# Recurrent outputs of batches 2 to 4 with tokens on partitions: transposes out, row-shifting transfers in

## Chip, cores and metric

The kernel runs on one core of a Trainium2 chip. The metric is the device time of one execution in microseconds, as the median of several runs. Engine names below: TensorE (PE), VectorE (DVE), ScalarE (ACT), GpSimd (POOL), SyncE (SP, which issues the transfers here).

## The reference

Two blocks follow each other. The first is a gated linear recurrence (mLSTM) over 4 batches of 8 heads, 768 tokens, head size 40:

```python
for t in range(S):
    m_new = np.maximum(f_gate[:, :, t] + m, i_gate[:, :, t])
    f_stab = np.exp(f_gate[:, :, t] + m - m_new); i_stab = np.exp(i_gate[:, :, t] - m_new)
    C = f_stab * C + i_stab * outer(v_t, k_t)        # a 40 x 40 state for each head
    n = f_stab * n + i_stab * k_t
    y[:, :, t] = sigmoid(o_t) * (C @ q_t) / max(abs(n . q_t), 1)
```

The heads side by side give x, 768 tokens x 320. The second block is u = x + Re(FFT over tokens and features of x), a layer norm, an MLP of width 1280 with ReLU, and out = u + MLP. All in 32-bit floats.

## The kernel before

**Chunks.** Tokens go in 6 chunks of 128 for each batch. Batch 1 (b = 0 in the code) works on whole chunks. Batches 2 to 4 (`plan_halves`) split each chunk in two halves of 64 tokens, so that all products of 64x64 or less run on four tiles of TensorE side by side. For each such chunk: scores of keys against queries (`halves_scores`), products of keys and weighted values which update the state (`halves_to_state`, `halves_add`), weights times scores (`halves_weigh`, VectorE), then the outputs: products from the state (`halves_from_state`) and from the chunk itself (`halves_from_chunk`, two turns with a small ScalarE copy, `halves_between`, in between).

**Outputs before.** A product has its stationary operand loaded into the array and its moving operand streamed. Before the change the stationary operand of an output is a 64-column slice of the state or a 41-column slice of the values (40 values and the column for n), and the moving one the 64 queries or weights. So the outputs lie in PSUM with head features on partitions and tokens along the row. `halves_gather` (ScalarE, `mlstm_heads`) copies them to SBUF, `halves_turn` turns them with four 128x128 transposes on TensorE (L681), and `mlstm_finish` (L684, VectorE) divides by the denominator, applies the output gate (tanh of half, `mlstm_tanh`) and writes x.

**Order of tokens.** The transform over tokens first folds token t with its mirror S - t: chunk pairs (0,5), (1,4), (2,3) (`mix_fold`). One chunk of each pair must lie backwards and shifted by one row. Before, these are chunks 2, 4 and 5 (`BACKWARDS`); the copy in `mlstm_heads` does the reversal and the shift, for free, as tokens lie along the row there. Rows whose token belongs to another chunk are copied one at a time (`h_first`).

**What sets the order.** The order is written by hand: `at(slot, phase, fn)` puts each step in a slot and a phase (EVAC 0, FILL 1, MAIN 2, FILL_PE 3), and the program is emitted in that order, so every engine works off its own instructions in it. For chunk c of a batch that starts at slot s0, s = s0 + 3c; scores stand at s, outputs at s + 3, the turn at s0 + (7, 10, 13, 16, 19, 19)[c], the finish one slot later. The MLP of batch 1 fills slots 31 to 62 (its products L1022, L1013, L1147), that of the next ones 32 slots each (`mlp_block` L1084, L1089; `mlp_out_pair` L1203). While a batch is in its MLP, the next one is in its recurrence. Second-layer weights arrive as 64-bit floats and are turned to 32 bits in five pieces (`Piece`: take and join on VectorE, convert on ScalarE) during batch 1's MLP.

**Queues and places.** All transfers are issued by SP in program order. Score tiles W have 3 buffers, gate inputs `so` 4. PSUM: scores and state products share one pair of banks, outputs and turned outputs another (`side(0)`, `side(1)`).

Of the kernel before, what the change touches and what calls it, by code (L numbers as in the profile page):

```python
# [10 lines left out]
FP = mybir.dt.float32  # L11
# [4 lines left out]
OP = mybir.AluOpType  # L16
# [24 lines left out]
BACKWARDS = (2, 4, 5)  # L41
PAIRS = ((0, 5), (1, 4), (2, 3))
ORDER = (0, 5, 1, 4, 2, 3)
M_INIT = -1.0e30
# [8 lines left out]
def kernel(  # L53
# [87 lines left out]
    def gates(gp):  # L141
# [44 lines left out]
        for t in hT_bufs + Cd_bufs:  # L186
            nc.gpsimd.memset(t, 0.0)
# [115 lines left out]

        def maxima_out():
            nc.sync.dma_start(out=M_d.rearrange("c i p t -> p c i t"), in_=M[0:BH].rearrange("p c (i t) -> p c i t", i=2))

        def halves_of_chunks(step):
# [8 lines left out]
            elif step == 1:  # L316
# [3 lines left out]
                nc.sync.dma_start(out=G_d[:, H:].rearrange("c p t -> p c t"), in_=g[H:BH])  # L320
# [12 lines left out]
            else:  # L333
                pt, pd = late["p2"]
                nc.vector.tensor_copy(out=colT[:, :, 1, H:], in_=pt[:, :, H:])  # L335
                nc.vector.tensor_copy(out=decB[:, NP:], in_=pd[:, NP:])

        at(12, FILL + 0.7, maxima_out)
        at(1, FILL + 0.2, parts, last)
# [9 lines left out]
        for n, (s, phase) in enumerate(((16, FILL + 0.2), (18, FILL + 0.3), (19, FILL + 0.4), (21, FILL_PE + 0.5),  # L349
                                        (26, FILL + 0.8))):  # L350
            at(s, phase, halves_of_chunks, n)
# [90 lines left out]
    def mlstm_queries(b, c):  # L442
        return slice(LH if b > 0 and c == 0 else 0, L)
# [40 lines left out]
    def mlstm_mask(b, c):  # L484
        for i in range(2):
            W = chunks[b, c].W[i * LH:(i + 1) * LH]
            nc.gpsimd.affine_select(out=W, in_=W, compare_op=OP.is_ge, fill=0.0, base=0, pattern=[[0, H], [1, LH]],  # L487
# [71 lines left out]
    def mlstm_heads(b, c, ph, parts=False):  # L559
# [3 lines left out]
        if b > 0:  # L563
            hT, before = (t.rearrange("p (hip m) t -> p hip m t", hip=2) for t in (hT, before))
        every, first, later = (tuple([slice(None)] * (len(ph.shape) - 1) + [t]) for t in
                               (slice(0, L), slice(0, 1), slice(1, L)))
        if c in BACKWARDS:
            nc.scalar.copy(out=hT[later], in_=backwards(ph, L - 1, L - 1))
            if c > TG:
                nc.scalar.copy(out=hT[first], in_=ph[first])  # L570
            else:
                nc.gpsimd.tensor_copy(out=k.hT[:, :, 0:1], in_=h_first)
        else:
            for r in (slice(hip * 64, hip * 64 + D1) for hip in range(2)) if parts else (slice(0, L),):
                nc.scalar.copy(out=hT[r], in_=ph[r])
            if c == 0:
# [869 lines left out]
```

## Time and profile before

| | us |
|---|---|
| median of 13 runs | 408.28 (403.96 to 411.09) |
| the profiled execution | 406.44 |
| its span in the profile | 404.7 |
| PE busy in 0 to 62.4 us: batch 1's recurrence and mix | 57.35 |
| PE busy in 62.4 to 117.7: batch 1 MLP, first layer; batch 2 recurrence | 51.70 of 55.30 |
| 117.7 to 171.7: second layer; batch 2 mix; batch 3 recurrence begins | 54.00 of 54.00 |
| 171.7 to 211.2: batch 2 MLP, first layer; batch 3 recurrence ends | 37.88 of 39.50 |
| 211.2 to 261.1: second layer; batch 3 mix; batch 4 recurrence begins | 48.84 of 49.90 |
| 261.1 to 300.4: batch 3 MLP, first layer; batch 4 recurrence ends | 37.80 of 39.30 |
| 300.4 to 341.0: second layer; batch 4 mix | 40.23 of 40.60 |
| 341.0 to 404.7: batch 4 MLP | 60.36 of 63.70 |

The profile is of one execution; its times are from the span's start. Busy times of TensorE are modelled from pipelined records, so the distance from one start to the next tells more than a record's duration. A wait is put down to the semaphore that came last.

### The profile page before, as it was taken

How to read it: one execution, taken by the hardware profiler on the slowest of the kernel's cores; microseconds unless marked ns; L12 is line 12 of the kernel's file. 1: busy time of each engine (PE TensorE's matmuls, PEld its weight loads, DVE VectorE, ACT ScalarE, POOL GpSimd, SP SyncE). 2: the span in 40 equal slices, each digit the busy share in tenths (PEclk: the TensorE clock that was granted, in tenths of full speed). 3: DMA queues.
4: the chain of work that ended last, by engine and by line, in shares of the span. 5: the costliest groups of instructions: out<-in, count | busy, mean ns of one | idle time of the engine just before them, and what ended most of it. 6: DMA issues, size and time to landing. Idle time of an engine off the chain costs nothing.

```text
span 404.7 us, 10669 instructions
## 1 busy us (share of the span) xinstructions
PE 388.2 (96%) x4246; PEld 283.8 (70%) x4246; DVE 280.2 (69%) x669; ACT 181.6 (45%) x510; POOL 131.6 (33%) x228
## 2 busy tenths in 40 slices
PE   8999999999899999998999999989999999999996
PEld 6877555556567677765559998856469997556996
DVE  8789976799748448576965579966764785436652
ACT  6987258587551242553472334644440023455000
POOL 5656314398952441240162424430220000020000
PEclk9999999999999999999999999999999999999999
DMA  7889599489555244365010644300000000000000
GB/s 211 283 233 324 118 237 266 128 250 246 152 150 144 64 138 124 92 188 153 0 43 3 168 112 144 101 3 2 0 2 16 18 35 32 0 2 0 32 34 32
DMA packets 23836, 43.29 MB, mean 107 GB/s; under 512 B 5076, under 2 KB 12972, under 8 KB 23660
## 3 DMA queue, kind: packets, MB, share of 16 engines
q1 hardware_dynamic: 23788, 42.63, 37.0%
q8 instruction: 33, 0.54, 0.6%
q14 instruction: 15, 0.12, 0.1%
HBM read 38.49 MB, written 4.12 MB: 105 GB/s over the span
## 4 chain that ended last, share of the span: by engine, by line
PE 80%; DVE 10%; issue 3%; ACT 3%; DMA 2%; POOL 1%; SPq 0%; POOLq 0%; DVEq 0%; ACTq 0%
PE po L1203 17%; PE pm L1084 17%; PE po L1147 8%; PE pm L1089 5%; PE pm L1022 5%; PE ph L491 4%; PE ps L491 3%; PE pu L901 3%; PE pz L870 2%; PE ph L681 2%; DMA qk<-in_qkT 2%; PE pm L1013 1%; PE put L944 1%; PE pz L858 1%; PE ph L532 1%
## 5 line engine op out<-in xcount | busy, mean ns | idle before, releaser
L1153 DVE SCALAR_TENSOR_TENSOR x<-po,rstd,x 128x160 f32<-128x160 f32 (+1 forms) x69 | 27.0, 395 | 38.0 <-PE po L1203 35.3
L1093 DVE TENSOR_TENSOR h<-h,pm 128x384 f32<-128x384 f32 x60 | 30.7, 550 | 31.1 <-PE pm L1084 17.1
L1084 PE MATMUL pm<-uT,w_sb 128*128 128x384 f32 x90 | 37.3, 501 | 0.2 <-DVE uT L1072 0.2
L464 ACT ACTIVATE W<-W,colT 128x64 f32<-128x64 f32 x144 | 37.4, 341 | 0.0
L1147 PE MATMUL po<-w_sb,h 128*128 128x320 f32 x120 | 34.4, 435 | 0.0
L629 POOL TENSOR_TENSOR C<-C,decB 128x164 f32<-128x164 f32 x30 | 17.1, 571 | 51.9 <-DVE C L638 47.7
L487 POOL TENSOR_SCALAR_AFFINE_SELECT W<-W 64x512 f32<-64x512 f32 x36 | 29.0, 806 | 15.2 <-ACT W L464 8.5
L1022 PE MATMUL pm<-uT,w_sb 128*128 128x384 f32 x80 | 29.9, 500 | 0.4 <-issue 0.2
L474 POOL TENSOR_TENSOR qg<-qk,Gb 128x512 f32<-128x512 f32 (+1 forms) x21 | 28.4, 1351 | 1.4 <-DMA Gb<-G_d 1.3
L1147 PEld LDWEIGHTS po<-w_sb,h 128*128 128x128 f32 x120 | 22.2, 190 | 9.4 <-issue 0.6
L1203 PE MATMUL po<-T,S 128*128 128x160 f32 x180 | 28.0, 302 | 0.3 <-DVE x L1153 0.3
L1203 PEld LDWEIGHTS po<-T,S 128*128 128x128 f32 x180 | 25.5, 190 | 1.8 <-DVE x L1153 0.5
L1203 PE MATMUL po<-w_sb,h 128*128 128x160 f32 x180 | 26.4, 301 | 0.0
L1203 PEld LDWEIGHTS po<-w_sb,h 128*128 128x128 f32 x180 | 25.1, 190 | 1.2 <-DVE x L1153 0.3
L1089 PE MATMUL pm<-uT,w1t_sb 64*128 64x384 f32 x120 | 25.4, 510 | 0.0
L968 POOL TENSOR_TENSOR t<-rstd 128x6 f32<-128x6 f32 x12 | 3.1, 256 | 65.3 <-DVE v L962 64.8
L1084 PEld LDWEIGHTS pm<-uT,w_sb 128*128 128x128 f32 x90 | 15.5, 189 | 12.5 <-DVE h L1093 3.6
L1140 ACT ACTIVATE h<-h 128x384 f32<-128x384 f32 x45 | 23.1, 520 | 2.0 <-DVE h L1093 2.0
L670 ACT COPY warm<-ph 1x1 f32<-1x1 f32 x18 | 2.6, 147 | 46.3 <-PE ph L491 42.8
L480 POOL TENSOR_TENSOR vw<-kvt,colT 128x328 f32<-128x328 f32 x23 | 18.6, 809 | 13.6 <-DVE colT L335 10.8
L949 ACT COPY uT<-put 128x384 f32<-128x384 f32 x24 | 11.1, 475 | 26.1 <-PE put L944 26.1
L937 ACT ACTIVATE uc<-x 128x384 f32<-128x384 f32 x24 | 14.6, 617 | 14.8 <-DVE x L929 14.8
(233 smaller groups left out, 878.8 us busy)
## 6 DMA issues: line engine op xcount, KB each, us to landing
kvt<-in_kv SPq DMA_DIRECT2D x24, 336.0 KB
qk<-in_qkT SPq DMA_DIRECT2D x48, 160.0 KB
raw<-in_w SPq DMA_DIRECT2D x10, 640.0 KB
Gb<-G_d SPq DMA_DIRECT2D x36, 128.0 KB
W<-M_d SPq DMA_DIRECT2D x36, 128.0 KB
so<-in_o SPq DMA_DIRECT2D x24, 160.0 KB
out<-x SPq DMA_DIRECT2D x24, 160.0 KB
ds_sb<-in_dft_s SPq DMA_DIRECT2D x1, 1155.0 KB
```

Of the source, the lines that this page charges most:

```text
L464: nc.scalar.activation(out=k.W[:, h, :], in_=M, func=AF.Exp, scale=-1.0, bias=colT[:, c, 0, b * H + h:b * H + h + 1])
L474: nc.gpsimd.tensor_tensor(out=k.qg[:, :, t], in0=k.qk[:, 0, :, t], in1=k.Gb[:, :, t], op=OP.mult)
L487: nc.gpsimd.affine_select(out=W, in_=W, compare_op=OP.is_ge, fill=0.0, base=0, pattern=[[0, H], [1, LH]], channel_multiplier=-1)
L491: nc.tensor.matmul(out, w, x, start=start, stop=True, skip_group_check=True)
L1022: nc.tensor.matmul(k.pm[i], w1_sb[:, ch, f0:f0 + L], u[2 * ch], start=(ch == 0 and not ahead), stop=(ch == 1 and ahead), skip_group_check= ...
L1084: nc.tensor.matmul(bank, w, u, start=start, stop=True, skip_group_check=True)
L1089: nc.tensor.matmul(bank, block(w1t_sb, i)[rows], mlp_u(gr, 1)[rows], start=False, stop=True, skip_group_check=True)
L1093: nc.vector.tensor_tensor(out=h, in0=h, in1=bank, op=OP.add)
L1140: nc.scalar.activation(out=h, in_=h, func=AF.Relu, scale=-1.0)
L1147: nc.tensor.matmul(k.po, hidden(gr, f)[:, i * L:(i + 1) * L], w2_sb[:, f, :], start=(f == 0), stop=(f == NFF - 1))
L1153: nc.vector.scalar_tensor_tensor(out=u, in0=po, scalar=k.rstd[:, c:c + 1], in1=u, op0=OP.mult, op1=OP.add)
L1203: nc.tensor.matmul(po, a[:, f], w[:, f], start=start and f == 0, stop=f == half - 1, skip_group_check=True)
```

## The change

For batches 2 to 4 the operands of the output products are exchanged: queries or weights are stationary (64 columns), the state or the values move (41 columns). The outputs then lie with tokens on partitions, and `mlstm_finish` reads them directly: the ScalarE copy, the four transposes and the second place in PSUM are gone. The finish stands at s + 4 (chunk 2 of batch 3: s + 5).

The reversal along tokens can no longer be done by a copy. The queries of backward chunks are loaded reversed (the host's layout), with maxima, decays and output gates reversed to match; the maxima and decays by copies on GpSimd and transfers to memory in four parts each. The backward chunks are now 0, 1 and 3, for batch 1 too. The shift by one row is made by transfers from SBUF to SBUF, 112 rows and 15 rows, in the new `halves_rows`, with single rows beside them. For odd head pairs the two halves of keys and values change places, so the state's sum reads its two banks crosswise.

Also: batches 3 and 4 start their recurrence at slots 53 and 83 (50 and 82), the output gates load a slot earlier, weights times scores stand earlier in batch 2, one piece of second-layer weights is converted a chunk earlier, two additions of the mix move.

```diff
-BACKWARDS = (2, 4, 5)
+BACKWARDS = (0, 1, 3)
...
 def halves_from_state(b, c):
-    k.ph = side(0)
...
-    product(k.ph[e * 64:(e + 1) * 64, hip, m, t], k.C[i][r, p * D1:p * D1 + LH], k.qg[r, p, t],
-            m == 0 and i == (c == 0))
+    k.ph = banks["heads"][:, :, 0:NP * D1].rearrange("p hip (m d) -> p hip m d", d=D1)
...
+    product(k.ph[t, hip, p, :], k.qg[r, p, t], k.C[i][r, p * D1:(p + 1) * D1], p == 0)
 def halves_from_chunk(b, c, turn):
...
-    product(k.ph[e * 64:e * 64 + n, hip, m, r], k.v[r, h * D1:h * D1 + n], k.W[r, h, :], False)
+    product(k.ph[queries(c, i), hip, p, :], k.W[rows(j), h, :], k.v[rows(j), h * D1:(h + 1) * D1],
+            2 * c + i == 0 and m == turn == 0)
-def halves_gather(b, c):
...
-def halves_turn(b, c):
-    k = chunks[b, c]
-    px = side(0 if c == NT - 1 else 1)
-    for p in range(NP):
-        nc.tensor.transpose(px[:, p // 2, p % 2], k.hT[:, p, :], ident)
-    k.px = px
 def mlstm_finish(b, c):
...
+    k.x = k.so if b > 0 and c in BACKWARDS else xs[b][:, c, 0:DM]
+def halves_rows(b, c):
+    x, y = xs[b][:, :, 0:DM], chunks[b, c].x
+    def move(out, in_):
+        nc.sync.dma_start(out=out, in_=in_)
+    if c == 2:
+        nc.gpsimd.tensor_copy(out=x[0:1, 1], in_=x[0:1, 2])
+        nc.gpsimd.tensor_copy(out=x[0:1, 2], in_=x[0:1, 0])
+        move(x[0:1, 0], chunks[b, 1].x[L - 1:L])
+    elif c in BACKWARDS:
+        n = L - L // 8
+        move(x[1:n + 1, c], y[0:n])
+        move(x[n + 1:L, c], y[n:L - 1])
+        if c != 1:
+            move(x[0:1, c], y[L - 1:L])
 def plan_halves(b, s0, stride=3):
...
-    at(s, FILL, mlstm_load_o, b, c)
+    at(s - 1, FILL, mlstm_load_o, b, c)
-    at(s + 1, MAIN + 0.7, halves_weigh, b, c)
+    at(s + 1, FILL + 0.55 if b == 1 and c > 0 else MAIN + 0.7, halves_weigh, b, c)
...
-    at(s + 4, FILL - 0.6, halves_gather, b, c)
-    at(s + 4, FILL + 0.35, mlstm_tanh, b, c)
-    t = s0 + (7, 10, 13, 16, 19, 19)[c]
-    at(t, FILL_PE + 0.5, halves_turn, b, c)
-    at(t + 1, MAIN + 0.55, mlstm_finish, b, c)
+    at(s + 3, FILL_PE + 0.6, mlstm_tanh, b, c)
+    at(s + (5 if (b, c) == (2, 2) else 4), FILL + 0.3 if b == 1 else MAIN + 0.55, mlstm_finish, b, c)
+    at(s + 6, FILL - 0.6, halves_rows, b, c)
...
-plan_batch(2, 50, 83, s_mlp + 2 * MLP_SLOTS)
-plan_batch(3, 82, 115, s_mlp + 3 * MLP_SLOTS)
+plan_batch(2, 53, 83, s_mlp + 2 * MLP_SLOTS)
+plan_batch(3, 83, 115, s_mlp + 3 * MLP_SLOTS)
...
-when += [((33, 0.7), (35, 0.7), (36, 0.6))] + [((s, 0.7), (s + 1, 0.7), (s + 2, 0.6)) for s in (36, 39, 42, 45)]
+when += [((33, 0.7), (34, 0.3), (34, 0.6)), ((34, 0.7), (35, 2.7), (36, 0.6))]
+when += [((s, 0.7), (s + 1, 0.7), (s + 2, 0.6)) for s in (36, 39, 42)]
```

## The prediction

> **What bounds the kernel now.** I read the page's busy shares first, then the busy time by stage, then who TensorE waited for, then TensorE's instructions in order of time around a few recurrence chunks, and last VectorE's in the stage in which it is fullest.
>
> ```profile
> PE 388.2 (96%) x4246; PEld 283.8 (70%) x4246; DVE 280.2 (69%) x669; ACT 181.6 (45%) x510; POOL 131.6 (33%) x228
> PE 80%; DVE 10%; issue 3%; ACT 3%; DMA 2%; POOL 1%; SPq 0%; POOLq 0%; DVEq 0%; ACTq 0%
> ```
> ```profile
> 62.40:117.70 55.30, 51.70 (x945) 31.19 (x943) 43.33 (x85) 37.21 (x112) 38.55 (x53) 1.00 0.74 204
> 117.70:171.70 54.00, 54.00 (x702) 39.40 (x700) 34.17 (x94) 18.74 (x61) 19.48 (x27) 1.00 0.39 110
> 171.70:211.20 39.50, 37.88 (x314) 21.53 (x306) 30.29 (x75) 21.34 (x59) 12.90 (x29) 1.00 0.34 94
> 211.20:261.10 49.90, 48.84 (x847) 45.80 (x846) 36.09 (x97) 19.27 (x62) 18.74 (x28) 1.00 0.39 110
> 261.10:300.40 39.30, 37.80 (x311) 21.51 (x304) 27.77 (x72) 19.38 (x50) 10.56 (x26) 1.00 0.02 5
> ```
> The columns after the stretch are its length, then busy PE, PEld, DVE, ACT, POOL, the granted clock and DMA. These five stages hold all the work that the change touches in batches 2 to 4: call them B, C, D, E, F. TensorE has no idle time in C and 1.1 to 3.6 us in the others, so a microsecond of TensorE work taken away is nearly a microsecond off the span, unless another engine was about as late. Its waits:
> ```profile
> PE ph L491 <- DVE x L703: 3.9, 5, 1.3
> PE ps L491 <- issue: 1.0, 1, 1.0
> PE pm L1013 <- issue: 0.8, 1, 0.8
> PE ph L491 <- ACT warm L670: 0.7, 1, 0.7
> PE ph L491 <- DVE W L643: 0.5, 1, 0.5
> ```
> The first line is D, E and F; the other four are B. In B, VectorE's order of time shows no idle time at all from 76.2 to 108.1 us: there it is as late as TensorE.
>
> **What a chunk costs on TensorE.** One chunk in order of time (start, duration, instruction; a 32-bit product leaves two records, a transpose one), then the same kinds in other shapes:
> ```profile
> 169.87 0.69 PE L491 MATMUL ph<-qg,C 40*64 40x64 f32 x32
> 170.38 0.41 PE L491 MATMUL ph<-W,kvt 64*41 64x64 f32 x16
> 170.61 0.65 PE L491 MATMUL ps<-qk 40*64 40x64 f32 x32
> 171.07 0.49 PE L491 MATMUL ps<-vw,kvt 64*40 64x41 f32 x32
> 171.38 0.41 PE L491 MATMUL ph<-W,kvt 64*41 64x64 f32 x16
> 171.72 1.56 PE L1084 MATMUL pm<-uT,w_sb 128*128 128x384 f32 x4
> 173.12 0.60 PE L681 MATMUL ph<-ident,h 128*128 128x128 f32 x4
> 173.55 0.49 PE L1084 MATMUL pm<-uT,w_sb 128*128 128x384 f32 x1
> ```
> ```profile
> 211.69 0.63 PE L491 MATMUL ps<-vw,kvt 64*64 64x41 f32 x32
> 212.25 0.54 PE L1203 MATMUL po<-w_sb,h 128*128 128x160 f32 x2
> ```
> The step from start to start is the price, since a record's own duration overlaps the next. Read: 16 products from the state 0.51 us, 8 from the chunk 0.23 us (0.34 us where full-array work follows, so that switch costs 0.11), and four transposes 0.43 us.
>
> **Removed: the turns.** 18 chunks x 4 transposes at 0.43 to 0.44 us a chunk: **7.9 us**, all between full-array products, so all on the path. With them go ScalarE's copies of the heads, 18 at 0.585 us and 12 small ones at 0.18, 12.7 us of an engine that is 45% busy: nothing by themselves, only less in front of its other copies.
>
> **Exchanged: stationary and moving operand.** 264 products from the state and 288 from the chunk now stream 41 columns and not 64. The favourable end: time goes with the moving columns. Scores against state products of this trace are 0.46 us at 64 columns and 0.31 at 41, 9.6 ns a product; 552 x 9.6 ns = 5.3 us saved. [...] The nearest row decides: the first chunk's state update already has the new shape, 64 stationary and 41 moving columns. It takes 212.25 - 211.69 = 0.56 us, less the switch 0.11: 0.45 us for 16. So narrow streaming buys little where 64 columns are loaded. From the state 0.51 -> 0.45 for 16, 16.5 times: 1.0 us; from the chunk 0.23 -> 0.225 for 8, 36 times: 0.2. I take **1.2 us** saved (ends -2.7 and +5.3).
>
> **Moved: the finish.** Before, products from the state of chunk c wait for the finish of chunk c-2, planned one slot ahead (for the last chunk less: slot s0+17 against the start of s0+18), and that finish waits for the turn. Now the finish of c-1 stands at s0+3c+1 and the products at s0+3c+3: two slots (2.0 us each in D and F, 2.8 in B, 4 and more in C and E) for five VectorE instructions, 0.16+0.17+0.20+0.64+0.49 = 1.7 us. The five waits, 3.9 us, should go. What is late next there is VectorE itself: in D from 171.8 to 179.5 us it has one gap of 0.24. I count two thirds, **2.6 us** (ends 0 and 3.9).
>
> **Weight conversion a chunk earlier.** In B, VectorE works off one conversion of 5 us per chunk without a gap. The new plan starts one of them in VectorE's idle stretches between 68 and 74 us (4.7 us in two waits), so VectorE is about 5 us less late, more than the about 2 us that TensorE loses there in work. Of B's 3.6 us of idle TensorE I count **0.7** (ends -1 and 3). Its load isn't later than now: the buffer is freed a chunk earlier as well. Weights a chunk earlier on VectorE (the product with the scores) are part of the same cover.
>
> **Added, at no cost, and what covers it.** Per batch nine row transfers: 112 and 15 rows for three chunks, single rows beside. None is on TensorE's path unless the fold waits for it. Tightest is chunk 3: issued at slot s0+15, folded at s0+18, so three slots, 5.9 us in D and F, 8.3 in B. From issue to landing, the trace has a gate transfer of 128 KB 1.8 us after its issue, and at the other end a 640 KB weight piece 6.3 us (59.92 to 66.20). 143 KB is nearest the first. Cost 0; at the far end under 1 us in D and in F. [...] On SP's queue that is 27 issues more, and six for the turned maxima and decays, at about 0.4 us: 1.2 us a chunk beside 4.4 us of issues in a period of 7.4. They wait for a finish planned two slots earlier; behind them stand the loads of a chunk four ahead, which already wait for buffers (W for TensorE, 35 us in all), and output stores. GpSimd: six one-row copies of 320 (a row of 161 takes 0.31, so 0.6 us each), less 6 small copies; four copies of the maxima in batch 1, about 1.5 us, ahead of a gate product which is done at 31.6 and used at 36.7 us; half-row swaps 0.7 us inside a wait of 2.4; two decay copies ahead of loads that have over 10 us. VectorE: two more small copies in its gap near 52 us. If these covers were gone, 1 to 2 us. Batches 3 and 4 start their recurrence three and one slots later; the last fold step then stands two and four slots ahead of the transforms, so this moves work and adds none.
>
> **Sum.** 7.9 + 1.2 + 2.6 + 0.7 = 12.4 us of the profiled 404.7 us span: 392.3. The profiled execution took 406.44, 1.74 over its span: 394.0. It was a run 0.45% under the median of 13 (408.28), so on the median's scale 394.0 x 408.28/406.44 = **395.8 us**.
>
> **Rivals.**
> 1. Streaming is what counts, and every wait goes: 7.9 + 5.3 + 3.9 + 2 = 19.1, span 385.6, time 389.1. Against it stands the 0.45 us row. Chance 0.14.
> 2. VectorE and GpSimd set the pace in B and D. For it: VectorE has no gap over 31 us in B, GpSimd none from 84 to 93; in D it takes over chunk 3's work, and 30.3 + 2.9 us in a stage of some 36 is 92%. Then the eight chunks or so of B and D return nothing, and the waits in D come back under other names: 7.9 x 10/18 + 0.6 + 1 = 6 us, span 398.7, time 402.2. Against it: the conversion brought forward. Chance 0.16.
> 3. Slower: the head outputs now have one place, which only VectorE's finish frees, for every one of 18 chunks; before, ScalarE's copy freed it, and the place read by VectorE was another. If VectorE is late each time as in its worst case now (1.27 us), TensorE idles 18 x 1.27 = 22.9 us. Span 404.7 - 9.1 - 3.9 + 22.9 = 414.6, time 418.2. It decides from (9.1 + 3.9)/18 = 0.72 us a chunk beyond the two slots. For it: rival 2's fullness. Against: in C and E two slots are 8 us. Chance 0.08.
>
> My forecast has 0.62, its own range 392 to 400. The range of 389 to 403.5 takes in most of rivals 1 and 2 and leaves out about 0.2. A measurement of this kernel can tell about 0.5% from no change: faster by more 0.87, within it 0.05 (rival 2 with costs of rival 3), slower 0.08.
>
> **What would show it.** Right: no transposes from the heads and about 8 us less of TensorE work between 62 and 300 us; no wait of head products for the finish above 1 us in all; products from the state still near 0.45 us for 16; stages C and E each about 2 us shorter, D and F about 3; nothing changed after the last batch's MLP starts. Wrong: state products at 0.33 us (rival 1); VectorE without gaps in B and D with TensorE waiting for its sums or weights (2); a wait for the finish at most chunks (3); VectorE or GpSimd waiting for row transfers ahead of the folds.

## The result

The kernel after takes **403.3 us** (median of 11 runs, 401.87 to 404.04) against 406.83 for the kernel before on the same chip; the ratio is 0.9908, interval 0.988 to 0.9936. So it is faster, by 3.5 us and not by the 12.4 forecast. (Each run below has its ratio to the kernel before on its own chip, so runs are compared by their ratios.) The profiled execution has a span of 400.5 us, 4.2 less than before.

Names in the profile's lines: `ps` and `ph` are the places in PSUM of scores and of head outputs, `pm` and `po` those of the MLP's two layers, `C` the state, `W` the weights, `uc` the normalised copy of a row of the mix, `x` a residual. First the page of the kernel after, engine totals and the chain's shares:

```profile
PE 382.5 (96%) x4174; PEld 278.4 (70%) x4174; DVE 278.9 (70%) x671; ACT 171.7 (43%) x481; POOL 131.9 (33%) x237
...
PEclk9999999979999999999999999999999999999999
...
PE 71%; DVE 17%; issue 4%; DMA 4%; ACT 2%; POOL 1%; SPq 0%; DVEq 0%; POOLq 0%; ACTq 0%
```

TensorE is busy 5.7 us less and ScalarE 9.9 us less: the turns and the copies are gone. (In work it is about 8.3 us less on TensorE: a stretch at half clock, shown below, made its products 2.6 us longer.) But TensorE's share of the chain of work fell from 80% to 71% and VectorE's rose from 10% to 17%: more of the time now passes through VectorE. And the row of the granted clock has a 7 in its ninth slice (80 to 90 us) where before there were only nines. By stage, the columns as before:

```profile
62.71:117.30 54.59, 50.95 (x865) 30.50 (x863) 44.51 (x89) 32.36 (x96) 33.51 (x50) 0.94 0.69 189
117.30:169.07 51.77, 51.77 (x629) 37.41 (x621) 31.24 (x86) 16.19 (x54) 16.73 (x23) 1.00 0.46 126
169.07:207.47 38.40, 36.72 (x418) 20.82 (x413) 28.66 (x76) 20.16 (x57) 15.49 (x33) 1.00 0.55 136
207.47:256.65 49.18, 47.64 (x714) 43.92 (x713) 35.28 (x100) 18.10 (x58) 16.63 (x25) 1.00 0.38 105
256.65:294.54 37.89, 36.40 (x415) 20.59 (x413) 28.40 (x72) 18.74 (x51) 15.11 (x32) 1.00 0.10 26
```

The borders are the same events as before (start of the first scores of batch 2, of the MLP's second layer of batch 1, of the first layer of batch 2, and so on), where before they lay at 62.44, 117.70, 171.72, 210.33, 261.14 and 299.55. B, of 55.26 us, became 54.59, and that although the first scores of batch 3 and the state products behind them (1.07 us) left it for C. Its clock is 0.94. The idle time of TensorE, length less busy time, is 3.60 us in B before and 3.64 after; over B to F together it is 7.8 before and 8.4 after. None of it went. TensorE's longest waits of the kernel after:

```profile
PE po L1237 <- DVE x L1187: 2.5, 3, 1.1
PE ps L519 <- DVE C L667: 1.9, 1, 1.9
PE ph L519 <- ACT warm L699: 1.6, 2, 1.3
PE pm L1118 <- DVE h L1127: 1.3, 2, 1.0
...
PE ph L519 <- DVE x L720: 1.0, 1, 1.0
```

The last line is the wait for the finish: 3.9 us before, 1.0 now. The four lines above it weren't there before, or were under 0.8 us. Lines two and three are stage B, and the place where they lie shows more than the sum. TensorE there, in order of time (start, duration, instruction, idle time before it and who ended it):

```profile
81.00 0.42 PE L519 MATMUL ph<-kvt,W 64*64 64x41 f32 x16
83.29 0.69 PE L519 MATMUL ps<-qk 40*64 40x64 f32 x32 [1.86 <-DVE C L667]
83.80 0.49 PE L519 MATMUL ps<-vw,kvt 64*40 64x41 f32 x32
85.64 0.67 PE L519 MATMUL ph<-kvt,W 64*64 64x41 f32 x16 [1.35 <-ACT warm L699]
...
86.93 4.82 PE L1056 MATMUL pm<-uT,w_sb 128*128 128x384 f32 x8
```

The scores of chunk 3 (c = 2) wait 1.86 us for VectorE's state add (L667), the second turn of chunk 2's outputs (L519, eight products of two records) waits 1.35 us for ScalarE's one-element read of the heads (`warm`, L699). Behind them eight products of 384 columns take 4.82 us; in run 11 below the same eight take 2.75, and the whole stretch from 85.64 to 91.69, 6.05 us here, takes 3.43 there. The clock in steps of 2 us tells why:

```profile
82.00:84.00 2.00, 0.71 (x53) 0.71 (x57) 1.71 (x5) 1.37 (x3) 0.69 (x2) 1.00 0.87 194
84.00:86.00 2.00, 0.65 (x46) 0.54 (x35) 2.00 (x2) 1.96 (x8) 2.00 (x2) 0.57 0.82 298
86.00:88.00 2.00, 2.00 (x17) 1.53 (x14) 1.90 (x5) 0.82 (x3) 1.91 (x2) 0.50 0.88 233
88.00:90.00 2.00, 2.00 (x4) 1.01 (x3) 1.50 (x3) 1.37 (x6) 1.16 (x2) 0.50 0.91 215
90.00:92.00 2.00, 2.00 (x6) 0.97 (x6) 1.74 (x6) 0.88 (x2) 0.20 (x1) 0.72 0.98 369
92.00:94.00 2.00, 2.00 (x9) 0.94 (x6) 2.00 (x2) 1.94 (x6) 2.00 (x2) 1.00 1.05 241
```

The column of the clock (after POOL) reads 1.00, 0.57, 0.50, 0.50, 0.72, 1.00. At the same place the kernel before has two shorter waits, and its clock stays 1.00:

```profile
81.03 0.44 PE L491 MATMUL ph<-W,kvt 64*41 64x64 f32 x16 [0.54 <-DVE W L643]
83.02 0.43 PE L491 MATMUL ph<-W,kvt 64*41 64x64 f32 x16 [0.75 <-ACT warm L670]
```

And what the two engines were waited for were doing, VectorE and then ScalarE:

```profile
79.06 0.68 DVE L672 TENSOR_TENSOR W<-ps,W 128x512 f32<-128x512 f32 x1
79.66 0.81 DVE L420 SCALAR_TENSOR_TENSOR e<-raw,e 128x640 uint32<-128x640 uint32 x1
80.39 0.82 DVE L422 SCALAR_TENSOR_TENSOR m<-raw,m 128x640 f32<-128x640 uint32 x1
81.25 0.82 DVE L426 TENSOR_TENSOR w_sb<-m,e 128x640 f32<-128x640 f32 x1
82.10 0.49 DVE L406 TENSOR_SCALAR e<-raw 128x640 uint32<-128x640 uint32 x1
82.51 0.49 DVE L408 TENSOR_SCALAR m<-raw 128x640 uint32<-128x640 uint32 x1
82.92 0.32 DVE L667 TENSOR_TENSOR C<-C,ps 128x164 f32<-128x164 f32 x1
```

```profile
82.63 0.83 ACT L413 ACTIVATE e<-e,ebias 128x640 uint32<-128x640 uint32 x1 [3.31 <-DVE e L406]
...
84.95 0.60 ACT L971 ACTIVATE uc<-x 128x384 f32<-128x384 f32 x1
85.45 0.13 ACT L699 COPY warm<-ph 1x1 f32<-1x1 f32 x1
```

VectorE has done the finish of chunk 1 and the weighing (L672), then joins one weight piece (L420, L422, L426) and takes the next (L406, L408) before it adds the state at 82.92. ScalarE stood 3.31 us ahead of its conversion (L413) for that take, and the one-element read is queued behind it in the same engine. One late engine holds up TensorE twice, by two ways. What has changed in VectorE's order is the place of the finish. The last instruction of the finish of chunk 1, before and after:

```profile
88.39 0.49 DVE L703 TENSOR_TENSOR x<-ph,so 128x320 f32<-128x320 f32 x1
78.65 0.49 DVE L720 TENSOR_TENSOR so<-ph,so 128x320 f32<-128x320 f32 x1
```

It is done nearly 10 us earlier, and the weighing behind it stands ahead of the weight piece, where before it stood behind (80.29 us).

### The profile page after: what moved, and what is told of

Same layout as the page of the kernel before. It is cut to its first block, busy times and chain, and to the rows that moved or that the text cites. A ratio compares the mean times of both kernels' runs of the same rounds, so it can differ in the third digit from the quotient of the medians.

```text
span 400.5 us, 10588 instructions
## 1 busy us (share of the span) xinstructions
PE 382.5 (96%) x4174; PEld 278.4 (70%) x4174; DVE 278.9 (70%) x671; ACT 171.7 (43%) x481; POOL 131.9 (33%) x237
## 4 chain that ended last, share of the span: by engine, by line
PE 71%; DVE 17%; issue 4%; DMA 4%; ACT 2%; POOL 1%; SPq 0%; DVEq 0%; POOLq 0%; ACTq 0%
PE po L1237 18%; PE pm L1118 15%; PE po L1181 8%; PE pm L1056 5%; PE pm L1123 4%; PE ph L519 4%; PE pu L935 3%; PE ps L519 2%; DMA Gb<-G_d 2%; PE pz L904 1%; DMA W<-M_d 1%; PE pz L892 1%; DVE h L1127 1%; PE put L978 1%; DVE so L716 1%
## 5 line engine op out<-in xcount | busy, mean ns | idle before, releaser
L652 POOL TENSOR_TENSOR C<-C,decB 128x164 f32<-128x164 f32 x30 | 15.7, 524 | 75.4 <-DVE C L667 64.2
L1118 PE MATMUL pm<-uT,w_sb 128*128 128x384 f32 x90 | 37.7, 506 | 2.1 <-DVE h L1127 1.3
L1056 PE MATMUL pm<-uT,w_sb 128*128 128x384 f32 x80 | 31.4, 530 | 0.1
L515 POOL TENSOR_SCALAR_AFFINE_SELECT W<-W 64x512 f32<-64x512 f32 x36 | 27.0, 749 | 13.4 <-ACT W L491 11.7
L1118 PEld LDWEIGHTS pm<-uT,w_sb 128*128 128x128 f32 x90 | 15.5, 189 | 16.4 <-DVE h L1127 7.5
L1123 PE MATMUL pm<-uT,w1t_sb 64*128 64x384 f32 x120 | 23.4, 508 | 0.0
L983 ACT COPY uT<-put 128x384 f32<-128x384 f32 x24 | 11.1, 476 | 27.7 <-PE put L978 27.7
L1056 PEld LDWEIGHTS pm<-uT,w_sb 128*128 128x128 f32 x80 | 15.2, 204 | 10.7 <-issue 3.2
```

The costliest lines, as they stand in the source:

```text
L1056: nc.tensor.matmul(k.pm[i], w1_sb[:, ch, f0:f0 + L], u[2 * ch], start=(ch == 0 and not ahead), stop=(ch == 1 and ahead), skip_group_check= ...
L1118: nc.tensor.matmul(bank, w, u, start=start, stop=True, skip_group_check=True)
L1123: nc.tensor.matmul(bank, block(w1t_sb, i)[rows], mlp_u(gr, 1)[rows], start=False, stop=True, skip_group_check=True)
```

## The experiments

Theory 1: TensorE's work was freed as forecast, and much of what is missing was lost in stage B, where the finish now stands earlier on VectorE, ahead of weight conversions and state adds; the other part went to waits for VectorE in stages E to G (G is what lies behind F). Rivals: the turns had been worth less than 7.9 us; the row transfers cost; the lower clock is the loss; the new places of the conversions are.

**1. The conversion schedule of before.** Of the change, only the weight pieces' slots are put back.

```diff
-    when += [((33, 0.7), (34, 0.3), (34, 0.6)), ((34, 0.7), (35, 2.7), (36, 0.6))]
-    when += [((s, 0.7), (s + 1, 0.7), (s + 2, 0.6)) for s in (36, 39, 42)]
+    when += [((33, 0.7), (35, 0.7), (36, 0.6))] + [((s, 0.7), (s + 1, 0.7), (s + 2, 0.6)) for s in (36, 39, 42, 45)]
```

> The changed kernel with the weight conversions at their old slots. Theory 1: conversion and finish both moved forward fill VectorE between 69 and 88 us; the scores of chunk 3 wait 1.9 us for its state sum, the second turn 1.4 for ScalarE behind a conversion, and TensorE then runs some 7 us at half clock. Then the waits shrink below 1.5 us together, no dip of the clock, and the time falls 3 to 5 us below the changed kernel's. Theory 2: the earlier finish alone fills VectorE, or the lateness comes later in the stage: within 1 us of the changed kernel, and the dip stays or moves.

Measured: 403.02 us, ratio 0.9925 (0.9893 to 0.9957), no difference from the kernel after. The waits are there under the same names (2.9 us in three for `warm`, 1.4 for the state add), and the clock is 0.50 to 0.54 from 84 to 90 us. The change had moved the last four pieces, not one, to earlier slots (34, 36, 39, 42 for 36, 39, 42, 45); that was neither the loss nor the gain of 0.7 us that the forecast had for it.

**2. The mix additions of before** (slots 4, 4, 5, 6, 8, 9 in batches 3 and 4).

```diff
-            add = [s_mix + c for c in ((4, 4, 5, 6, 7, 7) if b == 1 else (4, 5, 5, 6, 8, 9))]
+            add = [s_mix + c for c in ((4, 4, 5, 6, 7, 7) if b == 1 else (4, 4, 5, 6, 8, 9))]
```

> The changed kernel with the second addition of the mix back at its old slot (batches 3 and 4). Theory 1: that move puts two additions of 2.6 us each between finish, weights and residuals, and makes TensorE wait 1.5 us in the second layer of batch 2 and 1.0 in that of batch 3: 2 to 2.5 us less than the changed kernel. Theory 2: the waits are VectorE's total work there and come back at the next residual: within 0.7 us.

Measured: 403.97 us, ratio 0.9949 (0.993 to 0.9968): not better. The two waits for a residual in stage E and G (1.09, 1.01) give way to one of 2.72 us in E and one of 0.25 in G, as before the change: so the wait in G came from the moved addition, while in E it only took another shape.

**3. The kernel before without its turns.** This prices the removed work alone; the finish reads whatever lies there, and the place is set to zero once at the start.

```diff
-            nc.tensor.transpose(px[:, p // 2, p % 2], k.hT[:, p, :], ident)
+            pass
```

> The kernel before, leaving out the four transposes of each chunk of batches 2 to 4; the finish reads what lies in PSUM. Theory 1 (TensorE bounds, transposes are worth their 7.9 us): 7 to 11 us below the kernel before, as the finish no longer waits for a turn either. Theory 2 (VectorE and GpSimd are about as late): less than 4 us, with TensorE's idle time up by the rest.

Measured: 399.96 us, ratio 0.985 (0.9805 to 0.9894), 6.4 us less than the 406.38 of before on the same chip; span 397.3. The turns were worth four fifths of their TensorE time in the old schedule. By stage, B got 1.3 us shorter, C and D 3.2, E and F 2.1; of the 72 transposes of the kernel before 16 lie in B, 32 in C and D and 24 in E and F, which at 0.43 us for four is 1.7, 3.4 and 2.6. So the term of 7.9 us isn't what failed.

**4. The turns put back as useless work into the kernel after** (four transposes a chunk into unused columns of the heads' place, in the old slots).

```diff
+            at(s0 + (7, 10, 13, 16, 19, 19)[c], FILL_PE + 0.5, more_turns, b, c)
```

> The changed kernel with four transposes of an idle tile added for each chunk, at the slots of the old turns, into PSUM that nobody reads. Theory 1: the 14 chunks outside the stage of the conversions cost 0.44 us each: 6 to 8 us above the changed kernel. Theory 2: TensorE has room, under 4 us above it.

Measured: 433.94 us, ratio 1.0682 (1.0639 to 1.0725), far outside both. The waits say that the edit did something else as well:

```profile
PE ph L703 <- DVE x L724: 10.6, 6, 2.5
PE ph L703 <- DVE so L724: 8.4, 5, 3.1
```

L703 is the added transpose. It writes the place that the finish reads, and waits for it 11 times, 19.0 us. As a price of the turns it is inconclusive. It does show that a second writer of the heads' one place is dear; 12 of the 31 us that the run lost are not explained.

**5. The state add first.** In batch 2 the second state add of a chunk stands directly behind the weighing, ahead of the weight piece.

```diff
-                at(s + 1 + i, FILL - 0.2, halves_add, b, c, i)
+                at(s + 1, FILL + 0.56, halves_add, b, c, 1) if b == 1 and c > 0 and i else at(s + 1 + i, FILL - 0.2, halves_add, b, c, i)
```

> The kernel after, with one order changed: in batch 2 the second state add of chunks 2 to 6 stands on VectorE ahead of a weight piece's last three operations and of the next piece's first two, directly behind the chunk's weighing. Theory 1 (what cost the gain is a queue on VectorE: the scores of chunk 3 of batch 2 waited 1.86 us, at 83.29, for the state add, which stood behind those five operations): this wait goes. But the next wait in line, TensorE's second turn behind ScalarE's one-element read of the heads (1.35 us), stands behind the same piece's conversion on ScalarE, so part of it comes back there: I expect the two waits together to fall from 3.2 us to 1 to 3 us, and the time by 0 to 3 us against the kernel after (403.3). If the two together stay over 2 us the half clock behind them stays too. Rival (the waits are only slack that TensorE's clock limit would take anyway): the wait goes, and the time stays within 0.5 us.

Measured: 404.15 us, ratio 0.9947 (0.9918 to 0.9975). That is the order of the kernel before (80.29 and 80.89 us there). The wait for the state add is gone, and all of it and more came back in the other: TensorE stood 4.86 us for `warm` at 88.15 (I had expected 1 to 3 for both), with the clock at 0.5 until 92. (The 2 us in the expectation, over which the half clock was to stay, are an estimate of mine between the 1.29 us of waits before, at a clock of 1.00, and the 3.2 us of the kernel after, at 0.50.) With one of the two queues mended, the other takes it all.

**6. Both, and three weight pieces a slot later,** their conversion behind `warm`.

```diff
-    when += [((s, 0.7), (s + 1, 0.7), (s + 2, 0.6)) for s in (36, 39, 42)]
+    when += [((s, 0.7), (s + 1, 2.7), (s + 2, 0.6)) for s in (37, 40, 43)]
```

> The kernel after with the same state adds ahead, and the last three weight pieces one slot later, their conversion on ScalarE behind the one-element read of the heads and their last three operations on VectorE behind the chunk's finish, weighing and state add. Theory 1 (the queues on VectorE and ScalarE made the two waits of 1.86 and 1.35 us, and TensorE's idle time then brought the half clock that cost another 2.1 to 2.5 us): both waits fall under 0.5 us, the granted clock in 84 to 92 us is 1.00, and the time falls by 4 to 6 us against the kernel after, to 397.5 to 399.5. Theory 2 (VectorE is simply full from 69 to 88 us, and work put later comes due elsewhere): the waits appear at another place of the same stage, the gain is under 2 us.

Measured: 401.82 us, ratio 0.99 (0.9875 to 0.9925), no clear gain on the kernel after (0.988 to 0.9936): closer to theory 2. Both waits are gone, but the piece ahead of them was late as well, and with it a row of the mix that stands behind it, so TensorE waited 2.02 us for ScalarE's normalised copy (`put` <- `uc`) at 78.66, with the clock at 0.5 from 80 us. The piece had to move too (run 9).

**7. Useless products in the waits**, so that TensorE doesn't stand still.

```diff
+            if (b, c) == (1, 1):
+                at(s + 3, FILL_PE + 0.7, fill, 5)
+                at(s + 3, FILL_PE + 2.9, fill, 4)
```

> The kernel after, with nine products of 160 columns without use (about 0.30 us each, into unused columns of the heads' bank) in the queue of TensorE: five between the first turn of chunk 2 of batch 2 and the scores that wait 1.86 us, four ahead of the second turn that waits 1.35 us. The waits stay, but TensorE works through them. Theory 1 (idle TensorE makes the clock drop to half): the granted clock from 84 to 92 us is 1.00 and not 0.5, the eight products there take 2.75 us and not 4.8, and the time falls by 1.5 to 2.5 us against the kernel after, although nine products were added. Theory 2 (the half clock comes from something else, as a power limit): the clock drops as before, and the time stays or rises by up to 0.5 us.

Measured: 406.74 us, ratio 1.0013 (0.9992 to 1.0034). The products stood behind `warm`, which reads the same place, and waited 4.2 us for it: the place again, as in run 4. It says nothing of the clock; run 11 does it again in another place.

**8. No row transfers.**

```diff
-        k.x = k.so if b > 0 and c in BACKWARDS else xs[b][:, c, 0:DM]
+        k.x = xs[b][:, c, 0:DM]
...
-            at(s + 6, FILL - 0.6, halves_rows, b, c)
```

> The kernel after without the row-shifting transfers and row copies of batches 2 to 4 (12 transfers for each batch but the last rows, and the two copies of one row); the finish writes the backward chunks straight into the residual, so their tokens lie one row off, and the output isn't the reference's. Theory 1 (the row transfers are hidden, and what was lost was lost on VectorE): within 0.7 us of the kernel after. Theory 2 (the transfers delay what follows: the residual's additions, or they hold up SP's queue and slow VectorE's operations): faster by 1.5 us or more.

Measured: 406.41 us, ratio 1.0006 (0.9969 to 1.0043). It wasn't within 0.7 us, it was 1% slower than the kernel after. TensorE's waits in B are the same to the hundredth (1.86 and 1.35 us). The span is 3.7 us longer: 0.9 ahead of B, which the edit doesn't touch, a wait of 0.75 for a finish in D, and what is new in E:

```profile
247.30 0.49 DVE L720 TENSOR_TENSOR x<-ph,so 128x320 f32<-128x320 f32 x1 [1.96 <-DMA out<-x]
```

The finish now writes a backward chunk straight into the residual's tile, whose earlier contents are still on the way out; it waited 1.96 us for that store, and TensorE 2.37 us for the residual behind it (0.45 in the kernel after). So the run doesn't price the transfers alone. But in the kernel after no engine is put down as waiting for one of them, so they cost nothing that shows, and in E the detour through another tile, which they need, spares a wait.

**9. Four weight pieces later.** Run 6 with its earlier state adds (the edit of run 5), and the piece that stood ahead of the late mix row moved as well.

```diff
-    when += [((33, 0.7), (34, 0.3), (34, 0.6)), ((34, 0.7), (35, 2.7), (36, 0.6))]
-    when += [((s, 0.7), (s + 1, 0.7), (s + 2, 0.6)) for s in (36, 39, 42)]
+    when += [((33, 0.7), (34, 0.3), (34, 0.6))]
+    when += [((s, 0.7), (s + 1, 2.7), (s + 2, 0.6)) for s in (37, 40, 43, 46)]
```

> The kernel after with the second state add of chunks 2 to 6 of batch 2 directly behind the weighing, and the last four weight pieces (one more than in the run with three moved) three slots later, from the slot behind the chunk's finish on, their conversion on ScalarE behind the one-element read. No weight operation is then left on VectorE between 75 us and the second state add, and the residual that was late when three were moved (the wait of 2.02 us on ScalarE's normalised copy) has no piece ahead of it. Theory 1 (where the weight pieces stand on VectorE and ScalarE decides the waits of this stage, and with them the clock): the waits on the state add, on the one-element read and on the normalised copy fall under 1 us in sum, the granted clock is 1.00 between 80 and 96 us, and the time falls by 3.5 to 6 us against the kernel after, to 397.5 to 400. Theory 2 (VectorE is full in this stage wherever they stand): the waits come again at another place of the stage, 402 to 404 us.

Measured: 398.57 us, ratio 0.9775 (0.9717 to 0.9833), inside theory 1's window and clear of the kernel after (0.988 to 0.9936). The state adds alone had gained nothing (run 5); the pieces alone were not tried. Stage B ends at 114.9 us and not at 117.3. The same windows as above, in steps of 4 us:

```profile
80.00:84.00 4.00, 4.00 (x139) 2.89 (x138) 2.10 (x8) 3.31 (x10) 3.53 (x5) 1.00 0.85 185
...
88.00:92.00 4.00, 4.00 (x136) 2.63 (x136) 3.90 (x7) 2.76 (x9) 3.10 (x4) 1.00 0.94 268
108.00:112.00 4.00, 2.37 (x53) 1.45 (x52) 3.06 (x9) 1.36 (x5) 3.69 (x6) 1.00 0.93 219
112.00:116.00 4.00, 4.00 (x25) 1.88 (x24) 3.72 (x11) 1.99 (x7) 2.16 (x6) 0.57 0.96 246
```

TensorE has no idle time from 80 to 92 us and the clock is 1.00 there. The last of the moved pieces makes a smaller stall at 108 (TensorE busy 2.37 of 4 us), and the clock falls behind it.

**10. The finish behind the residual**, on top of run 9, for batches 3 and 4.

```diff
-            at(s + (5 if (b, c) == (2, 2) else 4), FILL + 0.3 if b == 1 else MAIN + 0.55, mlstm_finish, b, c)
+            at(s + (4 if b == 1 else 5), FILL + (0.3 if b == 1 else -0.5), mlstm_finish, b, c)
```

> As the run before it, and in batches 3 and 4 each finish stands on VectorE behind the residual of the next slot and not ahead of it. In the kernel after TensorE waited 1.09 us at 234.35, 0.45 at 246.75 and 1.01 at 321.03 for a residual that stood behind a mix add, a finish (1.7 us) and a weighing. Theory 1 (the finish in that place makes these waits): they go, and the time is 1.5 to 2.5 us under that of the run before it. Rival (the first product of the next chunk then waits for the later finish, since the heads have one place): a wait of the first state product on the finish of 0.5 to 1 us a chunk takes their place, and the time stays or rises by up to 4 us.

Measured: 403.63 us, ratio 0.9905 (0.9869 to 0.9941), 1.3% above run 9: the rival's side. The finish is later, but the residual stands in the middle of the slot (phase MAIN) and so still behind it: the waits for it stayed (3.1 us in three), and those for the finish grew from 2.0 to 3.0. Run 13 moves it really behind.

**11. Useless products in the waits, placed so that they wait for nothing.**

```diff
+                at(s + 3, FILL_PE + 0.3, fill, "heads", 256, 160, 6)
+                at(s + 3, FILL_PE + 2.9, fill, "scores", 420, 92, 6)
```

> The kernel after with products without use in TensorE's queue, this time ahead of the one-element read so that none waits for it: six of 160 columns (0.30 us each) into unused columns of the heads' bank ahead of the scores that wait 1.86 us at 83.29, and six of 92 columns (about 0.17 us each) into unused columns of the scores' bank ahead of the second turn that waits 1.35 us. Theory 1 (idle TensorE brings the half clock of 86 to 91 us, which made the eight products there take 4.8 us and not 2.75): the clock stays 1.00 through 80 to 92 us, those products take 2.8 us, and the time falls by 1.5 to 2.5 us against the kernel after although twelve products were added. Theory 2 (it has another cause): the clock falls to 0.5 as before, and the time is within 0.5 us or up to 1 us longer.

TensorE in order of time, L700 being the added products and L1064 the eight that took 4.82 us:

```profile
82.65 1.90 PE L700 MATMUL ph<-rest 128*128 128x160 f32 x12
84.59 0.69 PE L519 MATMUL ps<-qk 40*64 40x64 f32 x32
...
85.53 1.57 PE L700 MATMUL ps<-rest 128*128 128x92 f32 x12
87.04 0.44 PE L519 MATMUL ph<-kvt,W 64*64 64x41 f32 x16
...
87.79 2.75 PE L1064 MATMUL pm<-uT,w_sb 128*128 128x384 f32 x8
...
104.68 0.32 PE L519 MATMUL ph<-kvt,W 64*64 64x41 f32 x5 [1.54 <-issue]
```

Measured: 403.34 us, ratio 0.9892 (0.984 to 0.9944). The granted clock of the profiled execution is 1.000 (0.50 from 84.4 to 91.0 us in the kernel after), and the eight products take 2.75 us and not 4.82. So idle time did bring the half clock here, as theory 1 has it. But the time isn't shorter, where I had expected 1.5 to 2.5 us: stage B ends at 118.7 us. TensorE was 1.2 us ahead of the kernel after behind these products (91.31 us against 92.53). Then it stood 0.51 us for `warm` at 95.7, and 1.54 us at 104.7 in the middle of a group of eight products, a pause for which the profile names no engine ("issue"). So filling the waits gained nothing here, but how much the half clock costs by itself stays open: the added products took longer than the waits (1.94 and 1.51 us from start to start, against 1.86 and 1.35), and the last pause may have nothing to do with VectorE.

**12. The last four weight pieces not converted.**

```diff
-        for (s, phase), fn in zip(w, (p.take, p.convert, p.join)):
+        for (s, phase), fn in zip(w, (p.take, p.convert, p.join) if n < 6 else ()):
```

> The kernel after with the last four pieces of the second layer's weights not converted at all: their places hold zeros, so the output isn't the reference's; their loads stay. About 14 us of VectorE and 6 us of ScalarE work are gone from the stage between 73 and 100 us, and nothing else moves. Theory 1 (with this work there, the earlier finish made VectorE late, and that cost what the turns had freed): the stage ends 5 to 6.5 us earlier, the clock stays 1.00, and the time is 397 to 398.5 us, near that of the kernel before without its turns (399.96, a gain of 6.4 us). Theory 2 (the waits come from the order of the chunks, not from the weight work): under 2 us.

```profile
62.70:111.50 48.80, 48.37 (x868) 28.79 (x864) 27.65 (x70) 27.66 (x89) 31.43 (x52) 1.00 0.84 225
111.50:163.20 51.70, 51.70 (x624) 37.40 (x620) 31.25 (x86) 16.12 (x54) 16.48 (x22) 1.00 0.43 121
```

Measured: **396.13 us**, ratio 0.972 (0.9672 to 0.9768). Stage B lasts 48.8 us in place of 54.6 and TensorE idles 0.43 us in it; stage C is as long as in the kernel after (51.7). The two waits (3.2 us) and the time lost to the half clock (2.6) make up these 5.8 us. It is an upper bound on what the order can give, since 17 us of VectorE work left B here (44.5 to 27.7), and that could have helped the kernel before too.

**13. The finish really behind the residual** for three chunks of batch 4, on top of run 9.

```diff
+            f = (s + 5 if (b, c) == (2, 2) else s + 4, FILL + 0.3 if b == 1 else MAIN + 0.55)
+            at(*((s + 5, MAIN + 0.2) if b == 3 and c < 3 else f), mlstm_finish, b, c)
```

> The kernel with the state add first and four weight pieces later (398.57 us), and the finishes of chunks 1 to 3 of batch 4 now really behind the residual of the slot that follows (in the run that meant to do it they moved one slot, but still stood ahead of the residual, whose place is in the middle of the slot). Theory 1 (finish ahead of residual makes the waits in stage E): the waits of 1.09 us and 0.45 us for a residual in this stage go, the time falls by 1 to 1.5 us. Rival (VectorE is full there, or the first state product of the next chunk waits for the later finish): waits of the same size under another name, within 0.5 us, or up to 2 us longer.

Measured: 401.51 us, ratio 0.9845 (0.9808 to 0.9883), not better than run 9. The waits of 1.09 and 0.45 us in E go, and there come 0.84 and 0.58 for residuals, 0.60 for a mix addition and, at the border to F, 0.92 for the finish. The rival holds: VectorE is busy 15.2 of the 16 us between 232 and 248, and what is put last there is late.

**14. As 13, and the last weight piece behind the finish of its slot.**

```diff
-    when += [((s, 0.7), (s + 1, 2.7), (s + 2, 0.6)) for s in (37, 40, 43, 46)]
+    when += [((s, 0.7), (s + 1, 2.7), (s + 2, 0.6)) for s in (37, 40, 43)] + [((48, 0.58), (48, 2.7), (49, 0.65))]
```

> As the run before it, and the last weight piece stands behind the finish of its slot and not ahead of it (its first two operations were at 106.46 to 107.36 us ahead of that finish, for which TensorE waited 0.96 us, then 0.67 us for a weighing, and after which the granted clock in 112 to 116 us was 0.57). Theory 1 (each wait in this stage comes from where the weight pieces stand): these waits fall under 0.5 us, the clock stays 1.00, the time is 1.5 to 3 us under that of the run before it. Rival (GpSimd's mask and its square root are the late ones): the waits stay, within 0.5 us.

Measured: 399.76 us, ratio 0.9811 (0.9775 to 0.9848); beside run 13 the span is 2.9 us shorter, the intervals overlap. Stage B ends at 112.3 us (115.4 in run 13) and the clock is 1.00 from 104 to 120 us.

**15. The kernel before with four pieces later**, the same places as in run 9.

```diff
-    when += [((33, 0.7), (35, 0.7), (36, 0.6))] + [((s, 0.7), (s + 1, 0.7), (s + 2, 0.6)) for s in (36, 39, 42, 45)]
+    when += [((33, 0.7), (35, 0.7), (36, 0.6))] + [((s, 0.7), (s + 1, 2.7), (s + 2, 0.6)) for s in (37, 40, 43, 46)]
```

> The kernel before, turns and all, with its last four weight pieces at the later places that took 4.8 us off the kernel after. Theory 1 (the pieces had come to cost time only because the change put the finish ahead of them): within 1 us of the kernel before. Rival (the pieces stood badly from the first, and the change has nothing to do with it): faster by 3 us or more.

Measured: 409.41 us, ratio 1.005 (1.0022 to 1.0078): 0.5% slower than the kernel before; the waits for its finishes grew from 3.9 us in five to 7.0 in eight. The later places don't suit the old kernel, so the gain of run 9 isn't one that the kernel before had left lying. Run 9's other edit has no counterpart here: in the kernel before the state add already stands directly behind the weighing (80.89 and 80.29 us).

**16. Run 9 with the last piece as in run 14**, every finish where the kernel after has it.

> The kernel after with the state add of chunks 2 to 6 of batch 2 directly behind the weighing, three weight pieces later (from slots 37, 40, 43) and the last one behind the finish of slot 48; every finish is where the kernel after has it. The two runs before had the first layer's stage end at 115.4 us (last piece ahead of that finish) and 112.3 us (behind it), and the finish behind the residual cost about 2.5 us between 236 and 258 us. Theory 1 (order of the weight work on VectorE and ScalarE is what the change lost): the stage ends at 111.5 to 112.5 us, the span is 395 to 396, the time 396 to 398, close to the run without the four conversions (396.1). Rival (the gain at the stage's end is taken back by waits in the stages behind it): 398.5 us or more, as with the last piece ahead.

Measured: 398.37 us, ratio 0.9814 (0.9777 to 0.9851), span 396.9; stage B ends at 113.0. It falls between the two expectations and shows no difference from run 9, although B ends 1.9 us earlier. Waits of 0.48 us for the finish and 0.67 for a weighing are left at 108 to 110. Runs 9 and 16 do all the work of the kernel after, only in another order, and beat it and the kernel before.

## Why the prediction was wrong

**The turns: right.** 7.9 us of TensorE work, of which run 3 got 6.4 in the old schedule.

**Exchanged operands: wrong, most of the 1.2 us didn't come.** A chunk in the kernel after:

```profile
167.20 0.68 PE L519 MATMUL ph<-C,qg 40*64 40x41 f32 x32
167.69 0.42 PE L519 MATMUL ph<-kvt,W 64*64 64x41 f32 x16
167.92 0.67 PE L519 MATMUL ps<-qk 40*64 40x64 f32 x32
168.41 0.49 PE L519 MATMUL ps<-vw,kvt 64*40 64x41 f32 x32
168.72 0.42 PE L519 MATMUL ph<-kvt,W 64*64 64x41 f32 x16
169.07 0.59 PE L1118 MATMUL pm<-uT,w_sb 128*128 128x384 f32 x1
```

From start to start: 16 state products 0.49 us (0.51 before), 8 chunk products 0.23 (0.23), 16 scores 0.49 (0.46), and the whole chunk 1.87 us (1.85). At full clock TensorE's work in B to F fell by 8.5 us, where turns and operands together were to give 9.1. The row that I took as nearest, the state update with 64 stationary and 41 moving columns, had said 0.45. Streaming 41 columns and not 64 bought 0.02 us a group, so 9.6 ns a product (rival 1) was far off: with 64 stationary columns the count of moving ones hardly told here, as 16 scores with 64 moving ones cost the same 0.49 us. No run shows the other end, 2.7 us lost: in the kernel before a weight load of the chunk products took 114 ns with 41 columns and 134 with 64 (means of `ph<-W,kvt` by shape), and 8 of these products took 0.23 us before and after; in the trace the 32 loads of a group of state products lie beside its products (167.20 to 167.76 and 167.20 to 167.88).

**The finish waits: right by name, wrong in sum.** The wait for the finish fell from 3.9 us to 1.0, so 2.9 went where I had counted 2.6. But I had taken that as won. In E to G there are now 2.5 us of waits for residuals, against 0.3 before: the first, 1.09 us at 234.35, is for a residual that stands behind a mix addition, a finish and a weighing; the one of 1.01 at 321.03 is for one behind two mix additions. In F there is 1.05 us for the MLP's sums (`h`), which stand behind a finish and a weighing. An earlier finish is earlier than something. Runs 2, 10 and 13 moved the order of VectorE in E without gain; taking work off VectorE there wasn't tried, so that this is the cause in E and F is read from the traces and not shown by a run.

**Stage B: the step that failed.** The forecast had found VectorE as late as TensorE in B, and still booked TensorE's freed work there in full, and 0.7 us of idle time beside it, because the conversions a chunk earlier would make VectorE "about 5 us less late". That counted VectorE's total and not the order in which it works, and put at nothing what the moved finish does to the work that it passes. With one place for the heads the finish of chunk c has to be done before TensorE's outputs of chunk c + 1, so its 1.7 us move by more than a chunk (and the weighing by part of a slot) towards the front of a queue that is full from 69.2 to 88.2 us but for 0.3; joins and takes of weight pieces, state adds and, through ScalarE, the one-element read slide behind.

At full clock TensorE's work in B fell by 3.3 us (51.66 us before, 48.37 in run 12), 1.07 of it for the scores that left, but B became only 0.67 us shorter: the idle time stayed at 3.6, and the half clock took 2.6. Of the 3.6 us before, 2.0 were pauses for which the profile names no engine; the waits of 1.86 and 1.35 us came in the place of these and of the two shorter ones. Run 12 takes the conversions away and B loses 5.8 us; runs 9, 14 and 16 keep them, reorder them and B ends 2.4 to 5.0 us earlier; in run 15 the kernel before gains nothing by the later places.

So the order of VectorE's work behind the finish is shown as the cause in B. That it is the finish, rather than the weighing moved with it, which makes the old order bad is read from the order: no run puts one of the two back in batch 2.

How the missing 8.2 us of span split by stage, against the forecast's own sizes (C and E about 2 us shorter each, D and F about 3, so 2.4 left for B; in C and D, and in E and F, work moved over the border between them, so they are taken together):

| stage | expected | got | of the missing |
|---|---|---|---|
| B, with the scores that left it | 2.4 + 1.1 | 0.7 | 2.8 |
| C and D, with these scores | 5 - 1.1 | 2.5 | 1.4 |
| E and F | 5 | 2.1 | 2.9 |
| ahead of B, behind F | 0 | -1.1 | 1.1 |

By term it is plainer. Turns and operands gave 8.5 us of work of 9.1, so 0.6 are missing; of 3.3 us of idle time to be won (2.6 for the finish, 0.7 in B) none was won and 0.6 were added, which is 3.9; the half clock, which the forecast didn't have, took 2.6; and 1.1 lie ahead of B and behind F. Of these last, 0.76 is the residual at 321.03 (0.25 us before), which run 2 takes away again.

**The rivals.** The 403.3 us lie outside the forecast's own 392 to 400, and inside the wide range of 389 to 403.5 only at the end that rival 2 set. Rival 2, VectorE setting the pace in B and D (402.2 us), came nearest; it named the engine and was right for B; in C and D together 2.5 of 3.9 us came all the same. That it comes so near the time is in part luck: it didn't have the half clock. I gave it 0.16 because of the earlier conversion, and run 1 shows that this changed nothing. Rival 3, the heads' one place, isn't seen as waits for the finish (1.0 us in all), but by the program it is what the finish has to be early for: in run 10, with later finishes, these waits grew from 2.0 to 3.0 us. No engine waits for a row transfer, as forecast.

## What to carry over

A step that is moved ahead on a full engine delays all that it passes: list what stands behind it in that engine's order, and what stands behind that in the order of the engines that wait for it, before its own wait is booked as a gain. Where an engine has no gap, the order counts and not the busy share (runs 9 and 16, the work of the kernel after in another order: ratios 0.9775 and 0.9814 against 0.9908). After a change that turns the order of a queue, place the movable filler (here weight conversions) anew; run 15 shows that the new places would not have suited the old order.

## What the runs showed of the hardware

In two profiles the clock fell to half behind a wait of TensorE of about 2 us. In the kernel after the granted clock is 1.00 up to 84.2 us, 0.72 from there to 84.4 and 0.50 from 84.4 on, so it fell at 84.3 us, when only the wait of 1.86 us and 1.0 us of small products lay behind it; the wait of 1.35 us came after. In run 6 it is 0.88 from 78 to 80 us, 0.50 from 80 to 82 and 0.77 from 82 to 84, so it fell at 79.5 us, 0.8 us behind a single wait of 2.02. In the kernel before the two waits of 0.54 and 0.75 us left it at 1.00. The half clock lasted 6.8 us in the kernel after (84.3 to 91.1; 0.71 from 91.0 to 91.2) and 3.4 in run 6 (79.5 to 82.9). Run 11, with products in both pauses, kept 1.000 throughout. How long a wait it takes, what sets how long the half clock lasts, and whether power has a part in it, no run shows.
